# A decoder block with its gradients on one core: the last zero fill is moved to the end of GpSimd's queue and split unevenly over the transfer engines

## The chip, the core and the metric

The kernel runs on one core of one Trainium2 chip. A core has five engines with queues of their own: TensorE (PE in the profile, PEld for its weight loads), VectorE (DVE), ScalarE (ACT), GpSimd (POOL) and SyncE (SP). Data moves between the chip's memory and the core's on-chip buffer through sixteen transfer engines, which the profile calls DMA engines. GpSimd, SyncE and ScalarE only issue transfers; the sixteen carry them out. The metric is the time of one execution on the device, in microseconds (us), lower is better.

## The reference, cut to what matters

The program computes a forward pass of one token and all its gradients:

```python
mod = silu(c) @ w_mod                       # six vectors: sa, ca, ga, sb, cb, gb
h = layernorm(x) * (1 + ca) + sa
x = x + ga * attention(h, k_cache, v_cache, wq, wo)   # the last 4096 of 65536 rows alone
h = layernorm(x) * (1 + cb) + sb
x = x + gb * ((sigmoid(h @ w_gate) * (h @ w_up)) @ w_down)
...
_out, _vjp = jax.vjp(_f, x, k_cache, v_cache, wq, wo, w_gate, w_up, w_down, c, w_mod)
_grads = _vjp(grad_out)
return (_out, *_grads)
```

What matters here is the size of what goes out. The caches have 4 groups of 65,536 rows of 128 numbers in bf16. Only the last 4,096 rows of each group are read, so the gradients of both caches, `out_2` and `out_3`, are zero in the other 61,440 rows of each of the eight groups. These zeros have to be written: 126 MB of the 186 MB that the kernel writes. The rest is the gradients of the weights, of the 4,096 rows of each cache group, and a few vectors.

## The kernel before

**Work.** Everything that is read is loaded once and kept on chip, and stages follow one another in an order written out by hand: the modulation vectors and the query, attention scores, the folded products of the value cache and `wo`, the feed-forward block over seven column blocks of 512 (`turn`, loop at L1172), its gradients, the gradients of `wo`, `w_up`, `w_gate`, `w_mod` (`sec`, `s2`), `wq` (`dwq_tile`), and last the cache gradients: `grad_kv` makes 32 tiles for `out_3` (L1431) and 32 for `out_2` (L1481), and `kv_store` writes them group by group, 1 MB each.

**Queues.** Nearly all transfers are issued by GpSimd, in program order. SyncE issues some loads, and in the last stage part of the stores (`tail = nc.sync`, L1464): six 512-KB stores of L1312, two 1-MB stores of L1308, and the last three of the four `out_2` stores at L1304. The first of those four is the last transfer on GpSimd's queue. Each transfer of GpSimd's queue uses one of eight semaphores in turn, so it is issued only when the transfer eight before it has landed.

**Zero fills.** The zeros are cut into 120 pieces of 1 MB. `zero(n)` issues the next n pieces on GpSimd, and the tables `Z_...` at L49 to L59 say how many go out at each place of the program; a last call at L1485 would issue whatever is left. In this kernel nothing is left there: the last piece goes out at L1332 (`Z_ROWS[1]`), between the stores of the `w_up` gradient and those of the `wo` gradient. A piece is written in one of four ways:

- L209: from `zeros`, 128 rows of 2,048 one-byte zeros in the on-chip buffer, widened to 4 bytes on the way, so each of 128 rows becomes 8 KB, and each transfer engine writes eight of them (64 KB);
- L203 (`big`): from a part of the outputs that has been zeroed already (`zero_src`) to the output, 72 pieces;
- L194 and L197 (`narrow_`), for six pieces: the cursor that says which transfer engine comes next is set back (L192), then a small transfer of 5 rows of 256 bytes twice over goes out, and then 960 KB in 60 x 2 rows. The eight rows left out are written at L412 and L415;
- L201 (`uneven`): for the pieces whose number is in `UNEVEN`, which is empty here, so that it is never used.

The piece's number is worked out as `119 - len(zleft)` after it has been taken from the list, so 119 is the last of the 120.

**Lines that the change and the steps touch:** L39 and L59 (the tables), L171 to L183 (`uneven`), L185 to L211 (`zero`), L1332 (old place), L1130 and L1265 (the stores before and after it), L1304, L1308 and L1312 (the last stores), L1485 (new place), and L1511, the waits and the barrier that close the program.

Of the kernel before, what the change touches and what calls it, by code (L numbers as in the profile page):

```python
# [35 lines left out]
KIB = 512  # L36
SKIP = 4
NARROW = (15, 45, 75, 93, 103, 113)
UNEVEN = ()  # L39

def spread(total, n):
# [13 lines left out]
Z_FOLD = (1, 1, 2, 3)  # L56
Z_FFN = [(1, 0, 1)] + [(1, 1, 1)] * 4 + [(0, 2)]
Z_HAND = (1, 2, 1, 1, 1)
Z_ROWS = (1, 1, 0, 0, 0, 0, 0, 0)  # L59
JT = 3  # L60
JV = KD - JT
@with_exitstack
def kernel(
# [44 lines left out]
    def vt(shape, name, dt=FP32):  # L108
        return pool.tile(shape, dt, name=name)
# [4 lines left out]
    ZW = 4096  # L114
    zeros = vt([P, ZW // 2], "zeros", FP8)
# [55 lines left out]
    def uneven(piece):  # L171
        parts, at = [], 0
        flat_f = piece.rearrange("i x -> (i x)").bitcast(FP32)
        nc.gpsimd.inc_swdge_sem([], [], mode="reset_dge_cursor")
        for n, x in ((7, 16), (34, 512), (6, 16), (68, 512)):
            parts.append(nc.gpsimd.dma_start(
                out=flat_f[at:at + 2 * n * x].rearrange("(t p x) -> p t x", t=2, p=n),
                in_=zeros[0:n, 0:x].rearrange("p (t x) -> p t x", t=1).broadcast_to([n, 2, x])))
            at += 2 * n * x
        left = P * ZW // 2 - at  # L180
        nc.gpsimd.dma_start(out=flat_f[at:].rearrange("(p x) -> p x", p=16),
                            in_=zero_src.rearrange("i x -> (i x)")[0:left // 2].bitcast(FP8).rearrange("(p x) -> p x", p=16))
        return parts[0]  # L183

    def zero(n, after=None, big=False):  # L185
        for _ in range(n):
            if len(zleft) <= keep[0]:
                return
            region, narrow_ = zleft.pop(0)
            first = None  # L190
            if narrow_:
                nc.gpsimd.inc_swdge_sem([], [], mode="reset_dge_cursor")  # L192
                n = nlen - ncount.pop()
                first = nc.gpsimd.dma_start(  # L194
                    out=rest[0:NS, 0:nlen * 128].rearrange("p (t x) -> p t x", t=2)[:, :, n * 64:(n + 1) * 64],
                    in_=zeros[0:NS, 0:64].rearrange("p (t x) -> p t x", t=1).broadcast_to([NS, 2, 64]))
                ins = nc.gpsimd.dma_start(  # L197
                    out=region[8:P, :].bitcast(FP32).rearrange("(t p) x -> p t x", t=2),
                    in_=zeros[0:60, :].rearrange("p (t x) -> p t x", t=1).broadcast_to([60, 2, ZW // 2]))
            elif 119 - len(zleft) in UNEVEN:  # L200
                first = ins = uneven(region)  # L201
            elif big and region.shape[0] == 1:
                ins = nc.gpsimd.dma_start(  # L203
                    out=as_rows(region, BIGP).bitcast(FP32),
                    in_=zero_src[:, 0:P * ZW // 4].rearrange("i (p x) -> (i p) x", p=BIGP).bitcast(FP8))
            else:
                if region.shape[0] == 1:
                    region = as_rows(region, P)
                ins = nc.gpsimd.dma_start(out=region.bitcast(FP32), in_=zeros[:, :])  # L209
            if after is not None:  # L210
                dep(first or ins, after)  # L211
# [128 lines left out]
    def bcast(col_bf, ncols, out_bf, engs):  # L340
        for k, j0 in enumerate(range(0, ncols, 4)):
            ps = new_ps("bc_ps")
            for jj in range(4):
                nc.tensor.matmul(ps[:, jj * P:(jj + 1) * P],
                                 lhsT=col_bf[:, j0 + jj:j0 + jj + 1].broadcast_to([P, P]), rhs=ident_bf[:, :],
                                 start=(jj == 0), stop=(jj == 3), skip_group_check=True)
            o = out_bf[:, j0 * P:(j0 + 4) * P]
            if engs[k % len(engs)] == "A":
                last = nc.scalar.copy(out=o, in_=ps[:, :])
            else:  # L350
                last = cp(o, ps[:, :])
        return last
# [774 lines left out]
    def dw_rows(k, j, off, outer):  # L1127
        t = ar(off, 7)
        outer(t, h2[:, j:j + 1], dug_row[k])
        nc.gpsimd.dma_start(out=(dwu_view, dwg_view)[k][:, j, :], in_=t)  # L1130
# [94 lines left out]
    dw_rows(0, 1, 16, outer_dve)  # L1225
    zero(Z_ROWS[0])
    bcast(dattn_bf, KD, dattn_b, "V")
# [34 lines left out]
    def dwo(u):  # L1262
        for a in range(4):
            outer_dve(wo_t[u][:, a, :], o_perm[:, 8 * a + u:8 * a + u + 1], dattn_b)
        nc.gpsimd.dma_start(out=wo_dram(out_5, u), in_=wo_t[u])  # L1265
# [50 lines left out]
    for b in range(2):  # L1316
        do4 = new_ps("do4")
        for i in range(KD):
            for a in range(4):
# [4 lines left out]
                       in_=do4.rearrange("q (a h r) -> q a h r", a=4, h=4))  # L1324
# [6 lines left out]
    dw_rows(0, 2, 40, outer_dve)  # L1331
    zero(Z_ROWS[1])  # L1332
    dwo(2)
# [14 lines left out]
    dw_rows(0, 4, 32, outer_dve)  # L1348
    zero(Z_ROWS[2])
    dwo(3)  # L1350
    dw_rows(0, 5, 176, outer_dve)
    dw_rows(0, 6, 160, outer_dve)
    zero(Z_ROWS[3])
    dw_rows(0, 7, 40, outer_dve)
# [10 lines left out]
    dw_rows(1, 0, 64, outer_dve)  # L1365
    zero(Z_ROWS[4])
    dw_rows(1, 1, 72, outer_dve)
# [9 lines left out]
    dw_rows(1, 2, 80, outer_dve)  # L1377
    zero(Z_ROWS[5])
    dw_rows(1, 3, 88, outer_dve)
# [136 lines left out]
```

## Time and profile before

| | |
|---|---|
| median of 3 runs | 594.59 us (594.49 to 595.41) |
| the profiled execution | 594.85 us |
| its span in the profile | 593.0 us |
| busy: PE, DVE, ACT, POOL | 425.7, 354.7, 248.1, 145.9 us |
| moved in all | 246.58 MB, mean 416 GB/s |
| zero fills of L209, issue to landing | 42 of 1,024 KB, median 12.5 us |
| last issue on GpSimd, on SyncE | 560.75, 565.72 us |

The span is what the trace covers; the execution's own time is 1.85 us longer. The page divides the span into 40 equal slices and gives a digit for each engine: its busy share in tenths. The row DMA is the mean over the sixteen transfer engines. A queue's share in the table of queues is the time of its packets against sixteen engines' span; packets of one engine can overlap, so shares can add to more than the whole, and a stage's share can pass 1.00. In rows of the timeline come the start, the time taken, the engine, the line, the operation, and in brackets how long the engine stood idle before and what ended that. A group row gives the shortest, median and longest duration in ns and the first and last start. The trace also holds completion marks: for each transfer, the moment at which each of the sixteen engines reported its part as landed.

### The profile page before, as it was taken

The page shows a single profiled execution, that of the slowest core. Times are in us where ns is not written, and L with a number is a line of the kernel's source. Part 1 is how long each engine was busy: PE and PEld are TensorE (multiplying, and loading weights), DVE is VectorE, ACT ScalarE, POOL GpSimd, SP SyncE. Part 2 cuts the span into 40 slices and gives each one's busy share as a digit, 9 for nine tenths or more (in the row PEclk, how much of TensorE's full clock was granted, in tenths as well). Part 3 has the DMA queues.
Part 4 walks back from the last instruction along what each step waited for, and adds up shares of the span by engine and source line. Part 5 has one row for each costly group of instructions (what it writes and reads, how often), then busy time and mean ns, then how long its engine had stood idle before and what let it go on. Part 6 is the DMA issues. An engine that isn't in the chain of part 4 may idle for free.

```text
span 593.0 us, 10218 instructions
## 1 busy us (share of the span) xinstructions
PE 425.7 (72%) x4196; PEld 244.2 (41%) x4196; DVE 354.7 (60%) x647; ACT 248.1 (42%) x398; POOL 145.9 (25%) x250
## 2 busy tenths in 40 slices
PE   3997679999999999997975756776665457555300
PEld 2784433322334545643443545555452345131000
DVE  3765679988830102039272866887986868678700
ACT  2479511554540103411133646665672455563200
POOL 3113213112122212122222412323222432332100
PEclk9998889999999999999997757777787657555555
DMA  8999999999999999999999999999999999999996
GB/s 347 421 420 421 423 465 426 424 426 424 425 405 456 425 438 421 408 418 439 423 395 411 420 410 408 397 409 409 423 421 428 424 424 423 418 422 415 417 416 289
DMA packets 32047, 246.58 MB, mean 416 GB/s; under 512 B 4781, under 2 KB 4781, under 8 KB 16688
## 3 DMA queue, kind: packets, MB, share of 16 engines
q0 software_dynamic: 26864, 225.46, 94.3%
q1 hardware_dynamic: 5088, 20.46, 9.6%
q8 instruction: 33, 0.54, 0.4%
q14 instruction: 14, 0.11, 0.1%
q10 hardware_dynamic: 48, 0.01, 0.0%
HBM read 79.17 MB, written 185.60 MB: 446 GB/s over the span
## 4 chain that ended last, share of the span: by engine, by line
DMA 40%; PE 23%; DVE 19%; issue 5%; ACT 5%; POOL 1%; ACTq 0%; DVEq 0%; POOLq 0%; SPq 0%
DMA out_dram<-out_dram 12%; DMA out_dram<-arena 11%; PE n_ps L737 9%; DVE arena L249 7%; DMA arena<-in_w_mod_dram 6%; DMA arena<-in_B_w_gate_dram 5%; DVE arena L253 4%; PE t_ps L685 4%; DVE scr L253 3%; DMA out_dram<-zeros 3%; DMA arena<-in_B_w_down_dram 3%; PE b_ps L796 2%; ACT arena L524 2%; DVE arena L236 2%; PE tp_k L503 1%
## 5 line engine op out<-in xcount | busy, mean ns | idle before, releaser
L796 PE MATMUL b_ps<-arena 128*128 128x512 bf16 x512 | 116.3, 379 | 1.1 <-ACT arena L940 1.1
L236 DVE TENSOR_TENSOR arena<-arena 128x2048 bf16<-128x2048 bf16 x64 | 77.7, 1224 | 9.0 <-PE n_ps L737 5.3
L940 ACT COPY arena<-tp_side 128x1024 bf16<-128x1024 bf16 x62 | 60.9, 1017 | 49.7 <-PE tp_side L939 48.9
L796 PEld LDWEIGHTS <-arena 128*128 128x128 bf16 x512 | 48.3, 98 | 56.6 <-issue 2.9
L737 PE MATMUL n_ps<-arena 128*128 128x512 bf16 x256 | 67.6, 388 | 3.6 <-DVE arena L236 3.3
L203 POOL DMA_DIRECT2D out_dram<-out_dram x72 | 35.6, 495 | 128.8 <-PE n_ps L737 52.4
L939 PE MATMUL tp_side<-ident_bf,arena 128*128 128x128 bf16 x496 | 50.6, 268 | 10.4 <-DVE arena L236 6.0
L939 PEld LDWEIGHTS <-arena 128*128 128x128 bf16 x496 | 41.7, 123 | 19.4 <-issue 8.9
L693 ACT CAST arena<-t_ps 128x512 bf16<-128x512 f32 x56 | 28.9, 598 | 39.9 <-PE t_ps L685 39.9
L253 DVE CUSTOM_DVE_ANT_0 arena<-arena,scr 128x1024 bf16<-128x1024 bf16 x35 | 40.8, 1220 | 0.2
L209 POOL DMA_DIRECT2D out_dram<-zeros x42 | 23.1, 554 | 55.0 <-DVE rows_all L236 25.1
L1295 PE MATMUL ps_kv<-arena 32*128 32x512 bf16 x64 | 25.2, 584 | 15.6 <-DVE arena L257 9.5
L253 DVE CUSTOM_DVE_ANT_0 scr<-arena,b1k 128x1024 bf16<-128x1024 bf16 x28 | 34.2, 1222 | 3.4 <-DMA arena<-in_B_w_down_dram 3.0
L1299 ACT ACTIVATE arena<-ps_kv 128x512 bf16<-128x512 f32 x48 | 25.0, 723 | 26.7 <-PE ps_kv L1295 17.1
L737 PEld LDWEIGHTS <-arena 128*128 128x128 bf16 x256 | 21.4, 99 | 35.8 <-issue 19.5
L249 DVE TENSOR_SCALAR arena<-arena,h 128x3584 bf16<-128x3584 bf16 (+1 forms) x24 | 28.3, 1192 | 12.0 <-DMA out_dram<-arena 12.0
L245 DVE CAST arena<-b_ps 128x512 bf16<-128x512 f32 x6 | 4.1, 692 | 48.8 <-PE b_ps L796 48.8
L685 PE MATMUL t_ps<-arena 128*32 128x512 bf16 x256 | 24.1, 399 | 2.8 <-ACT arena L760 2.8
L524 ACT COPY arena<-tp_wq 128x1024 bf16<-128x1024 bf16 x23 | 21.4, 1070 | 7.3 <-PE tp_wq L522 7.3
L1077 ACT COPY arena<-tp_ug 128x1024 bf16<-128x1024 bf16 x21 | 20.5, 1007 | 7.0 <-PE tp_ug L1076 7.0
L965 POOL DMA_DIRECT2D arena<-in_B_w_up_dram x14 | 10.7, 765 | 40.1 <-DVE dh2acc L253 26.7
L1295 PEld LDWEIGHTS <-arena 32*128 32x128 bf16 x64 | 6.8, 114 | 32.9 <-issue 32.0
(326 smaller groups left out, 664.4 us busy)
## 6 DMA issues: line engine op xcount, KB each, us to landing
out_dram<-zeros POOLq DMA_DIRECT2D x42, 1024.0 KB, 12.5
out_dram<-arena POOLq DMA_DIRECT2D x34, 1024.0 KB, 16.4
out_dram<-arena POOLq DMA_DIRECT2D x16, 896.0 KB, 17.1
arena<-in_A_wq_dram POOLq DMA_DIRECT2D x8, 1024.0 KB, 21.0
arena<-in_A_wo_dram POOLq DMA_DIRECT2D x8, 1024.0 KB, 13.8
arena<-in_w_mod_dram POOLq DMA_DIRECT2D x7, 1024.0 KB, 19.0
arena<-in_B_w_up_dram POOLq DMA_DIRECT2D x14, 512.0 KB, 9.9
arena<-in_B_w_gate_dram POOLq DMA_DIRECT2D x14, 512.0 KB, 14.6
```

Source lines behind the costliest of these rows:

```text
L203: ins = nc.gpsimd.dma_start(out=as_rows(region, BIGP).bitcast(FP32), in_=zero_src[:, 0:P * ZW // 4].rearrange("i (p x) -> (i p) x", p=BIGP ...
L236: return nc.vector.tensor_tensor(out=out, in0=a, in1=b, op=op)
L249: return nc.vector.tensor_scalar(out=out, in0=a, scalar1=s1, scalar2=None, op0=op0)
L253: return nc.vector.tensor_tensor_reduce(out=out, in0=w, in1=b, scale=1.0, scalar=0.0, op0=ALU.mult, op1=ALU.add, accum_out=acc)
L524: nc.scalar.copy(out=blk, in_=tp[:, :])
L685: nc.tensor.matmul(ps[32 * hh:32 * hh + 32, :].rearrange("p (j m) -> p j m", j=4), lhsT=N_sb[:, h * P + a:(h + 1) * P - 3 + a:4], rhs=a4[: ...
L693: nc.scalar.copy(out=o, in_=v)
L737: mm = nc.tensor.matmul(nbank[k][:, :], lhsT=k_nat[:, g, t_ * DH:(t_ + 1) * DH], rhs=vp[:, t_ % 2, 4 * k:4 * k + 4, :].rearrange("p h d -> ...
L796: mm = nc.tensor.matmul(bbank[p][k][:, :], lhsT=a4[:, p, h, :], rhs=wo_t[u][:, a, k * 512:(k + 1) * 512], start=(i == 0 and a == 0), stop= ...
L939: nc.tensor.transpose(tp[:, i * P:(i + 1) * P], blk[:, i * P:(i + 1) * P], ident_bf[:, :])
L940: nc.scalar.copy(out=blk if dst is None else dst, in_=tp[:, :])
L1295: nc.tensor.matmul(ps[:, :], lhsT=rows[r, t8 * P:(t8 + 1) * P], rhs=bd[r, :], start=True, stop=True, tile_position=(32 * tc_, 0))
```

## The change

Three places change. The fill at `Z_ROWS[1]` is left out at L1332, so one piece is still in the list at the end, and the call at L1485 issues it behind all other entries of GpSimd's queue. That piece has number 119, which is now in `UNEVEN`, so it goes through `uneven`. And `uneven` itself is cut in another way.

```diff
-UNEVEN = ()
+UNEVEN = (119,)
...
-Z_ROWS = (1, 1, 0, 0, 0, 0, 0, 0)
+Z_ROWS = (1, 0, 0, 0, 0, 0, 0, 0)
...
         nc.gpsimd.inc_swdge_sem([], [], mode="reset_dge_cursor")
-        for n, x in ((7, 16), (34, 512), (6, 16), (68, 512)):
+        for n, t, x in ((7, 2, 16), (2, 12, ZW // 2), (6, 2, 16), (4, 12, ZW // 2)):
             parts.append(nc.gpsimd.dma_start(
-                out=flat_f[at:at + 2 * n * x].rearrange("(t p x) -> p t x", t=2, p=n),
-                in_=zeros[0:n, 0:x].rearrange("p (t x) -> p t x", t=1).broadcast_to([n, 2, x])))
-            at += 2 * n * x
+                out=flat_f[at:at + t * n * x].rearrange("(t p x) -> p t x", t=t, p=n),
+                in_=zeros[0:n, 0:x].rearrange("p (t x) -> p t x", t=1).broadcast_to([n, t, x])))
+            at += t * n * x
         left = P * ZW // 2 - at
         nc.gpsimd.dma_start(out=flat_f[at:].rearrange("(p x) -> p x", p=16),
                             in_=zero_src.rearrange("i x -> (i x)")[0:left // 2].bitcast(FP8).rearrange("(p x) -> p x", p=16))
```

The piece goes out as a reset of the cursor and five transfers: 7 rows of two 64-byte parts, 2 rows of twelve 8-KB parts, 6 rows of two 64-byte parts, 4 rows of twelve 8-KB parts, and the remaining 457,088 bytes in 16 equal parts of 28,568 bytes, which are copied from `zero_src`. If rows go to successive transfer engines from engine 0 on, the first transfer takes engines 0 to 6, the second 7 and 8, the third 9 to 14, and the fourth 15, 0, 1 and 2. Those six write 96 KB and the sixteenth of the rest; the other ten write the sixteenth of the rest and at most some 64-byte parts.

## The prediction

> **What bounds the kernel now.** I read the page first (slices and queues), then the last microseconds by stage, then GpSimd's queue around the moved fill, and last the closing instructions.
>
> ```profile
> DMA  8999999999999999999999999999999999999996
> GB/s 347 421 420 421 423 465 426 424 426 424 425 405 456 425 438 421 408 418 439 423 395 411 420 410 408 397 409 409 423 421 428 424 424 423 418 422 415 417 416 289
> q0 software_dynamic: 26864, 225.46, 94.3%
> q1 hardware_dynamic: 5088, 20.46, 9.6%
> ```
>
> The sixteen transfer engines are busy from the first slice to the last but one; no compute engine is above 72%. The kernel ends when the last of the sixteen has written its last byte. GpSimd's queue (q0) carries 225 of 247 MB, SyncE's (q1) 20. Only the last slice is loose:
>
> ```profile
> 584.00:585.00 1.00, 0.00 (x0) 0.00 (x0) 0.00 (x0) 0.00 (x0) 0.00 (x0) 0.50 1.04 434
> 585.00:586.00 1.00, 0.00 (x0) 0.00 (x0) 0.00 (x0) 0.00 (x0) 0.00 (x0) 0.50 0.94 393
> 586.00:587.00 1.00, 0.00 (x0) 0.00 (x0) 0.00 (x0) 0.00 (x0) 0.00 (x0) 0.50 0.87 369
> 587.00:588.00 1.00, 0.00 (x0) 0.00 (x0) 0.00 (x0) 0.00 (x0) 0.00 (x0) 0.50 0.81 344
> 588.00:589.00 1.00, 0.00 (x0) 0.00 (x0) 0.00 (x0) 0.00 (x0) 0.00 (x0) 0.50 0.43 180
> 589.00:590.00 1.00, 0.00 (x0) 0.00 (x0) 0.00 (x0) 0.00 (x0) 0.00 (x0) 0.50 0.25 107
> 590.00:591.00 1.00, 0.00 (x0) 0.00 (x0) 0.00 (x0) 0.00 (x0) 0.00 (x0) 0.50 0.08 33
> ```
>
> The last two columns are the share of the sixteen engines and GB/s. From 585 to 591 the shares add up to 3.38 of 6 us: on average an engine is idle for the last 2.6 us. That is all that any balancing can win. Which engines are idle, the trace's completion marks tell: each transfer leaves one mark from each engine (in order of time, without the engine's number). The last transfer of GpSimd's queue (L1304, issued at 560.75) and the last of SyncE's (L1304, issued at 565.72):
>
> ```
> GpSimd 575.71 575.86 579.34 579.63 579.82 580.02 | 580.57 581.08 581.12 581.44 581.83 581.84 582.66 583.71 584.47 584.51
> SyncE  585.60 585.76 588.09 588.19 588.38 588.39 | 588.44 588.73 588.80 589.20 589.36 589.43 590.12 590.26 591.23 591.27
> ```
>
> Six engines lead. They already do at the old place of the fill, where the L1130 store before it has marks at 464.70 to 465.19 for six and 466.02 to 468.77 for ten. At the end the six are through by 588.39 (mean 587.4), the ten by 591.27 (mean 589.7). From the last mark to the end of the span are 1.77 us of closing waits.
>
> **Does the change feed those six?** Its pieces go to positions 7, 8, 15, 0, 1, 2 if, as the code's narrow fills suppose, a transfer of n rows takes the next n engines from a cursor that was reset to engine 0. At the narrow fill of 328 us the trace has five pairs of 256-byte pieces (L194, engines 0 to 4): three are followed by marks of the leading six (335.14, 335.95, 336.45), two by marks of the ten. In its 960-KB part (L197, which skips engine 4) the mark without 64 KB before it is one of the ten. So three of the six are among engines 0 to 3, as wanted of 0, 1, 2; for 7, 8 and 15 only the count fits (three of the six are outside 0 to 4).
>
> **The change part by part.** *Removed:* the fill at L1332, the L209 row in
>
> ```profile
> 458.62 0.61 POOL L1130 DMA_DIRECT2D out_dram<-arena  x1 [3.58 <-DVE arena L249]
> 459.23 0.80 POOL L209 DMA_DIRECT2D out_dram<-zeros  x1
> 460.20 0.62 POOL L1265 DMA_DIRECT2D out_dram<-arena  x1 [0.18 <-issue]
> 530.38 0.53 POOL L1304 DMA_DIRECT2D out_dram<-arena  x1 [1.66 <-DMA out_dram<-arena]
> 551.39 0.90 POOL L1308 DMA_DIRECT2D out_dram<-arena  x1 [1.92 <-DVE arena L249]
> 560.75 0.53 POOL L1304 DMA_DIRECT2D out_dram<-arena  x1 [8.46 <-DVE arena L249]
> ```
>
> It costs each engine 64 KB: its first mark is 2.45 us after that of the store before (464.70 to 467.15), its last 2.46 (468.77 to 471.23). The 44 transfers behind it on GpSimd's queue move up by 2.45 us; so do SyncE's 14 behind 536 us, because the stores wait for DVE, and DVE waits for buffers that these transfers free. No engine runs dry: when L1265 is issued at 460.20, the earliest engine still has work until 464.70. So this is worth nothing by itself: the same 1 MB follows later.
>
> *Added:* behind the last store (560.75, then about 558.3) a cursor reset (18 ns on its six earlier occasions) and five issues at 0.53 to 0.67 us each (rows L209, L194, L197), some 3 us of GpSimd, beside 30 us of transfers. Each waits for the transfer eight before it: the 530.38 row starts 0.28 us after the last mark of that one (530.10). For the fourth and fifth that is 570.29 and 573.15, less 2.45: they are issued near 568 and 571. GpSimd's queue holds work on the earliest engine until 575.71 less 2.45 = 573.3, and SyncE's beyond 583: hidden. Without that cover an engine would stand idle for up to the 2.9 us between those two marks.
>
> Engine time, six engines: 12 pieces of 8 KB at the fill's own rate, 96/64 x 2.45 = 3.68; a sixteenth of the rest, 28,568 bytes at the 2.43 us which a 64-KB piece of L203 takes, 1.06; less 2.45: **+2.29 us**. Ten engines: 1.06 - 2.45 = **-1.39 us**. Four extra transfers on every engine: an L194 transfer leaves marks 0.16 to 0.24 us after those before it where it carries nothing, but L194 and L197 together took 2.45 us on the first engine at 424 us (430.88 to 433.33), no more than one full transfer. So between 0 and 0.8 us; I take 0.1, since the pair is the nearest row. Small pieces out of few partitions: L412 (23 KB per engine from 16 partitions) took 0.93 us where the fill's rate gives 0.86; at worst 8% of 3.68, 0.3 us, on the six; I take 0.
>
> The six then end at 588.39 + 2.29 + 0.1 = 590.8, the ten at 591.27 - 1.39 + 0.1 = 590.0. The six are now last, the end moves from 591.27 to 590.8: **-0.5 us**. With both bounds against it, 588.39 + 2.29 + 0.8 + 0.3 = 591.8, +0.5. The span would be 592.5 and its execution 594.85 - 0.5 = 594.35. That execution stands 0.26 above the median of the runs, so the time is 594.59 - 0.5 = **594.1**.
>
> [...]
>
> **The rivals.**
> *The ten set the end* (593.2). If the six take up part of their extra 60 KB beside SyncE's queue and gain more than 0.8 us on my sum, the end is the ten's, 591.27 - 1.39: 594.59 - 1.39. For it: at GpSimd's last transfer the lead is 4.4 us in the mean, against 2.3 at SyncE's, so the lead depends on how the two queues share an engine; and the shares above 1.00 show pieces that overlap. Against it: engines that have only one queue left move 64 KB in 2.45 us too.
>
> *GpSimd's closing drain becomes the last* (596.2, slower).
>
> ```profile
> L1511 SPq EVENT_SEMAPHORE  x11: 17/28/28, 576.6 to 593.0; - x11
> L1511 POOLq DRAIN  x3: 51/102/26978, 560.7 to 592.8; - x3
> ```
>
> The long drain runs from 560.73 to 587.71, 3.2 us beyond the last mark of GpSimd's queue (584.51); SyncE's own waits end at 592.2. Today 4.5 us of room. The change puts GpSimd's pieces last on six engines. If they land with SyncE's last, near 590.7, the drain ends at 593.9, 1.7 us beyond 592.2: 594.59 + 1.6. It decides once GpSimd's last mark is beyond 589. Against it: at half shares (64 KB took 4.85 us on the earliest engine, 570.86 to 575.71) the four later of the six need 577.6 + 7.4 + 2.1 = 587.1.
>
> *One of the six fed engines is not a leading one:* 591.27 + 2.29 = 593.56, so 596.9. Against it: the three leading engines found among 0 to 3. This is also how the change would not do what it says.
>
> *The middle runs dry without the fill:* at most its 2.45 us come back, 594.1 + 2.45 = 596.5; against it the 4.5 us of stock at 460.20.
>
> *Each small transfer takes the slot of a full one* (603.9): the engine waits for each transfer's mark before it begins the next, so four more cost four spacings of 2.45 us: 594.1 + 9.8. L194's marks all but exclude it. [...]
>
> **Chances.** Forecast 0.52, own range 593.3 to 595.1 (both bounds, and run to run differences of the tail); the ten set the end 0.23; the drain 0.10; a wrong engine 0.09; a dry middle 0.04; a slot each 0.02. A measurement tells about 0.2% (1.2 us) from no change: faster is below 593.4, slower above 595.8. Faster: 0.20 of the second case (some of it lies nearer) and 0.07 of the forecast's lower edge, 0.27. Slower: drain, wrong engine, dry middle, a slot each, less 0.02 of the drain that costs under 1.2 us: 0.23. Same: 0.50. The range reaches to 592.8, the second case with 0.4 us of slack, and to 596.3, which takes in the drain and half of the dry middle; it leaves out the wrong engine and the slot each.
>
> **What would show it.** Right: SyncE's last transfer has its six leading marks up by over 2 us against the ten's and a total spread of under 3 us (5.67 now); the DMA share stays near 1 until about 589 and falls at once; L1304 on GpSimd starts near 558.3; the marks of the ten end near 590. Wrong: a lone mark beyond 592 (a wrong engine), a drain of GpSimd that ends behind SyncE's waits, stores that start later than 558.3 plus 1 us (nothing moved up), or small transfers of the fill whose marks are 2 us apart.

## The result, and the profile after

| | before | after |
|---|---|---|
| median | 595.0 us of 4 runs (594.49 to 595.49) | 603.06 us of 4 runs (602.62 to 603.52) |
| ratio | | 1.0136 (95% interval 1.0118 to 1.0153) |
| the profiled execution, its span | 594.85, 593.0 us | 603.52, 601.5 us |
| last mark of GpSimd's queue | 584.51 | 597.38 |
| last mark of SyncE's queue | 591.27 | 596.31 |
| end of the span behind the last mark of all | 1.8 us | 4.1 us |

The changed kernel is 1.4% slower, about 8 us, where 0.5 us less was forecast. The bytes are the same, but the table of the page that counts packets is not. First the page of the kernel before, then that of the changed one (the row DMA is the busy share of the sixteen engines in tenths, in 40 slices):

```profile
DMA packets 32047, 246.58 MB, mean 416 GB/s; under 512 B 4781, under 2 KB 4781, under 8 KB 16688
```

```profile
DMA  8999999999999999999999999999999999999992
GB/s 353 420 417 421 424 451 438 418 429 413 442 427 439 415 423 441 433 406 419 419 434 377 421 406 397 405 413 410 421 425 424 427 421 412 422 413 412 412 407 87
DMA packets 32447, 246.58 MB, mean 410 GB/s; under 512 B 5221, under 2 KB 5221, under 8 KB 17128
q0 software_dynamic: 27264, 225.46, 93.1%
```

Up to the last slice little has changed: 407 GB/s in the 39th, against 416. The last slice moves 87 GB/s where it moved 289. And there are 400 packets more, all on GpSimd's queue (26,864 to 27,264). The changed kernel from 586 to 598 us by stage (the last two columns are the share of the sixteen engines and GB/s):

```profile
586.00:588.00 2.00, 0.00 (x0) 0.00 (x0) 0.00 (x0) 0.00 (x0) 0.00 (x0) 0.50 1.05 399
588.00:590.00 2.00, 0.00 (x0) 0.00 (x0) 0.00 (x0) 0.00 (x0) 0.00 (x0) 0.50 0.50 195
590.00:592.00 2.00, 0.00 (x0) 0.00 (x0) 0.00 (x0) 0.00 (x0) 0.00 (x0) 0.50 0.29 100
592.00:594.00 2.00, 0.00 (x0) 0.00 (x0) 0.00 (x0) 0.00 (x0) 0.00 (x0) 0.50 0.06 25
594.00:596.00 2.00, 0.00 (x0) 0.00 (x0) 0.00 (x0) 0.00 (x0) 0.00 (x0) 0.50 0.11 39
596.00:598.00 2.00, 0.00 (x0) 0.00 (x0) 0.00 (x0) 0.00 (x0) 0.00 (x0) 0.50 0.00 0
```

A share of 0.06 is one engine of sixteen. So fifteen engines are through near 592.6, and one writes on for another 5 us. The starts of its 8-KB packets show what it still has on both queues, and that these take turns on it one for one:

```
SyncE   591.25 591.87 592.50 593.12 593.74 594.36 594.98
GpSimd  591.60 592.22 592.84 593.46 594.09 594.71 595.33
```

Each takes 0.32 to 0.35 us, where 0.31 is the usual time in the kernel before, so by then this engine is hardly slow any more: it is behind. The completion marks say the same on both queues (in order of time, one per engine, without its number):

```
SyncE, last transfer  586.71 587.22 587.35 587.37 587.40 588.22 588.26 589.12 589.16 589.25 589.30 589.66 591.03 591.05 591.54 596.31
GpSimd, fill part 1   575.64 576.22 579.00 579.50 579.55 579.62 579.66 579.74 579.85 580.46 581.01 582.58 582.61 582.81 582.85 583.03
GpSimd, fill part 2   577.92 582.63 582.66 582.89 583.16 583.28 583.32 583.67 584.04 584.79 586.30 586.39 586.42 586.65 586.71 588.29
GpSimd, fill part 4   586.11 586.88 587.05 587.39 587.53 587.55 587.57 588.41 588.44 589.31 589.36 589.45 591.24 591.25 591.73 596.49
GpSimd, fill part 5   587.78 587.81 588.31 588.43 588.46 588.50 588.74 589.34 589.40 590.25 590.28 590.37 592.10 592.14 592.59 597.38
```

Two things stand in these rows. The lone engine is late with SyncE's store too (596.31 against 591.54), so it is that engine that is behind and not only its part of GpSimd's queue. And part 2, which has pieces for two engines alone, took 3.6 to 3.8 us of most of the others (580.46 to 584.04 and 582.58 to 586.30, for example, matched in order of time, with the marks of part 2 one place on).

The issues of the changed kernel on GpSimd's timeline (start, us, engine, line, operation, in brackets the idle time before):

```profile
558.15 0.53 POOL L1304 DMA_DIRECT2D out_dram<-arena  x1 [7.79 <-DVE arena L249]
558.75 0.60 POOL L176 DMA_DIRECT2D out_dram<-zeros  x1
560.01 0.63 POOL L176 DMA_DIRECT2D out_dram<-zeros  x1 [0.66 <-DMA out_dram<-arena]
564.31 0.54 POOL L176 DMA_DIRECT2D out_dram<-zeros  x1 [3.67 <-DMA out_dram<-arena]
568.02 0.64 POOL L176 DMA_DIRECT2D out_dram<-zeros  x1 [3.17 <-DMA out_dram<-arena]
571.09 0.53 POOL L181 DMA_DIRECT2D out_dram<-out_dram  x1 [2.44 <-DMA out_dram<-arena]
```

They are as forecast: the last store moved from 560.75 to 558.15, and the last piece is issued at 571.09, 4 us ahead of the first mark of that store. Nothing is late on the issuing side. The closing groups of the changed kernel (ns shortest, median and longest, then first and last start):

```profile
L1511 POOLq DRAIN  x3: 46/93/29672, 571.1 to 601.2; - x3
L1511 SPq DRAIN  x3: 7/7/7, 598.3 to 601.0; - x3
```

GpSimd's long drain begins behind its last issue and takes 29.67 us: to 600.74, 3.36 us behind the last mark of its queue. SyncE's own waits are over at 598.3. Before, the drain had ended 4.5 us ahead of them.

The span grew by 8.5 us: 5.0 by the lone engine (597.38 against 592.42, where it ends in the run `spread_rows` below, which lacks it), 1.1 from 591.27 to 592.42, and 2.4 behind the last mark (4.14 against 1.77).

### The profile page after: what moved, and what is told of

Its sections match the earlier page's. It is cut to its first block, busy times and chain, and to the rows that moved or that the text cites. A ratio compares the mean times of both kernels' runs of the same rounds, so it can differ in the third digit from the quotient of the medians.

```text
span 601.5 us, 10194 instructions
## 1 busy us (share of the span) xinstructions
PE 425.4 (71%) x4167; PEld 243.5 (40%) x4196; DVE 354.6 (59%) x647; ACT 248.0 (41%) x398; POOL 149.0 (25%) x254
## 3 DMA queue, kind: packets, MB, share of 16 engines
q0 software_dynamic: 27264, 225.46, 93.1%
## 4 chain that ended last, share of the span: by engine, by line
PE 39%; DMA 21%; DVE 20%; issue 7%; ACT 6%; POOL 2%; ACTq 0%; POOLq 0%; DVEq 0%
PE b_ps L796 14%; DMA out_dram<-arena 12%; PE n_ps L737 9%; DMA arena<-in_B_w_gate_dram 5%; DVE arena L236 4%; DVE arena L253 4%; PE t_ps L685 4%; DVE arena L249 3%; DVE scr L253 3%; DMA out_dram<-out_dram 3%; ACT arena L524 2%; PE tp_side L939 1%; PE tp_k L503 1%; PE w_ps L466 1%; PE fg L1053 1%
## 5 line engine op out<-in xcount | busy, mean ns | idle before, releaser
L737 PE MATMUL n_ps<-arena 128*128 128x512 bf16 x246 | 66.3, 389 | 3.8 <-DVE arena L236 3.0
L939 PE MATMUL tp_side<-ident_bf,arena 128*128 128x128 bf16 x496 | 48.7, 262 | 11.6 <-DVE arena L236 5.8
L1053 PE MATMUL fg<-arena,h_bf 128*32 128x256 bf16 x224 | 15.1, 404 | 7.3 <-DMA arena<-in_B_w_gate_dram 7.3
```

The lines of the kernel that those rows point to most:

```text
L737: mm = nc.tensor.matmul(nbank[k][:, :], lhsT=k_nat[:, g, t_ * DH:(t_ + 1) * DH], rhs=vp[:, t_ % 2, 4 * k:4 * k + 4, :].rearrange("p h d -> ...
L939: nc.tensor.transpose(tp[:, i * P:(i + 1) * P], blk[:, i * P:(i + 1) * P], ident_bf[:, :])
```

## Experiments

All kernels are variants of the changed one, and each diff is against it. Ratios are to the kernel before, run beside it on the same chip; "filler" is explained under `tiny_pieces`.

| run | what of the change is in it | median us | ratio, 95% interval | last mark GpSimd, SyncE |
|---|---|---|---|---|
| move_only | the move, even fill | 596.31 | 1.0022 (1.0012 to 1.0033) | 586.74, 591.01 |
| split_only | the five transfers at the old place | 597.93 | 1.0053 (1.0034 to 1.0072) | 587.50, 593.96 |
| before_store | all, ahead of the last store | 602.89 | 1.0133 (1.0115 to 1.0152) | 597.37, 596.46 |
| five_even | five transfers, even, no fillers | 596.90 | 1.0038 (1.0022 to 1.0054) | 588.62, 592.85 |
| one_piece | five transfers, even, from memory | 596.83 | 1.0034 (1.0021 to 1.0047) | 587.15, 591.41 |
| fat_pieces | uneven, few fillers, from memory | 596.56 | 1.0027 (1.0015 to 1.0039) | 588.34, 592.51 |
| tiny_pieces | even, all fillers | 599.38 | 1.0078 (1.0059 to 1.0096) | 593.12, 590.65 |
| spread_rows | all, other rows of `zeros` | 598.55 | 1.0062 (1.0047 to 1.0077) | 592.42, 591.37 |

Four more kernels held the fill back until SyncE's last store had landed; they show the fill alone, each was run once, and they are told below.

### Place or shape: move_only, split_only, before_store, isolated

The move without the new shape:

```diff
-UNEVEN = (119,)
+UNEVEN = ()
```

> The last fill goes to the end of GpSimd's queue, but in one even transfer (L209), as it was at its old place. Theory A (the split is at fault: in the changed kernel one transfer engine leaves its last marks at 596.49 and 597.38, the next one at 592.59): no lone late mark, the last fill's marks spread over less than 7 us, GpSimd's last mark before 589, time 593.5 to 595.5. Theory B (the place is at fault: whatever stands last on GpSimd's queue lands late beside SyncE's stores, and GpSimd's drain ends 3.3 us behind its last mark): GpSimd's last mark beyond 592, time above 599.

Measured: 596.31 us (594.56 to 597.09, 10 runs), 0.22% slower, and no lone mark: SyncE's last marks run from 586.20 to 591.01 and none stands alone at the end (590.64, 590.69, 591.01), and GpSimd's drain ends 3.2 us behind 586.74 and so ahead of SyncE's waits. So moving the fill costs some 1.5 us (theory A's range is missed by 0.8), and it isn't what makes the 8 us. Where the 1.5 us come from stays open: the execution that was profiled took 594.56, the fastest of the ten, and shows no reason.

The new shape at the old place:

```diff
-Z_ROWS = (1, 0, 0, 0, 0, 0, 0, 0)
+Z_ROWS = (1, 1, 0, 0, 0, 0, 0, 0)
```

> The last fill stays at its old place (L1332) and is cut into the five uneven transfers there. Theory A: the engine with too much is behind from then on, every later transfer of the queue lands late on it, time 598 to 602. Theory B: nothing small is at the tail, the drain ends before SyncE's waits as before, time 593.5 to 596.

Measured: 597.93 us, and neither theory had this. No engine is late at the end, nor behind the fill (part 5 has marks from 466.59 to 470.96, in line with the store before it, 464.57 to 468.87). SyncE's queue moves no packet there between 422 and 543 us, so the fill meets no second queue; whether that is why the source rows cost nothing there wasn't tried. The timeline of GpSimd at the old place shows a third thing:

```profile
459.30 3.29 POOL L176 DMA_DIRECT2D out_dram<-zeros  x4
462.58 0.77 POOL L181 DMA_DIRECT2D out_dram<-out_dram  x1
464.88 0.59 POOL L1265 DMA_DIRECT2D out_dram<-arena  x1 [1.54 <-DVE arena L249]
467.30 0.77 POOL L1265 DMA_DIRECT2D out_dram<-arena  x1 [1.82 <-DVE arena L249]
469.41 2.88 POOL L1265 DMA_DIRECT2D out_dram<-arena  x1 [1.35 <-DVE arena L249]
```

The stores of L1265 were issued at 460.20, 461.79 and 463.47 in the kernel before. They come 4.7 to 5.9 us later. The brackets name DVE, but each starts 0.54 to 0.60 us behind the last mark of the transfer eight before it (464.28, 466.73, 468.87): the five small transfers have taken five of the eight places that the queue has in flight, where in the kernel before the place for 460.20 had been free since 454.99. In the stage from 470 to 472 us the DMA share is 0.95 at 397 GB/s, against 1.00 at 414 before: in the middle of the program the stock does run thin. SyncE's last store goes out at 568.38, 2.7 us later than the 565.72 before, which is most of the 3.1 us. Ahead of work that still has to be issued, these five transfers cost more than one; that their number does it, and not their shape, is argued from the eight places, since five even transfers were not run there.

The fill one store earlier, so that a 1-MB store and not the fill is the last entry of the queue:

```diff
+    keep[0] = 0
+    zero(len(zleft))
     for g in range(G):
         kv_store(out_2, dk_home, g, nc.gpsimd if g < 1 else tail)
-    keep[0] = 0
-    zero(len(zleft))
```

> The uneven fill is issued just ahead of the out_2 store (L1304), not behind it, so that GpSimd's queue ends with an even store. Theory A: same load of each engine, time 600 to 604. Theory B: the fill's small transfers run while GpSimd waits for that store's data, its last mark comes before 589, the drain is covered, time 594 to 597.

Measured: 602.89 us, the changed kernel's time, and again one engine alone: 596.46 on SyncE's queue, the next at 591.17. So being the very last entry isn't the cause.

The fill by itself: `zero` is handed SyncE's last store and waits for it.

```diff
-        queue.dma_start(out=kv_out(og, g), in_=home[:, g, :])
+        return queue.dma_start(out=kv_out(og, g), in_=home[:, g, :])
...
-        kv_store(out_2, dk_home, g, nc.gpsimd if g < 1 else tail)
+        last_store = kv_store(out_2, dk_home, g, nc.gpsimd if g < 1 else tail)
...
-    zero(len(zleft))
+    zero(len(zleft), last_store)
```

> The changed kernel, with the uneven fill held back until SyncE's last store has landed, so that it runs alone and its marks show what each engine carries. If six engines have 12 pieces each (theory B, the split does what it says): two engines late by about 3.7 us in the second transfer, four others by about 3.7 us in the fourth, all sixteen within 5 us of each other at the end. If one engine is in both (theory A): one mark about 7.4 us behind the ten that have none. Time 600 to 606 by either.

Measured: 606.1 us in one run. Its timeline on GpSimd, and its last stages:

```profile
590.15 2.42 POOL L176 DMA_DIRECT2D out_dram<-zeros  x4 [30.59 <-DMA out_dram<-arena]
592.54 0.56 POOL L181 DMA_DIRECT2D out_dram<-out_dram  x1
```

```profile
594.00:596.00 2.00, 0.00 (x0) 0.00 (x0) 0.00 (x0) 0.00 (x0) 0.00 (x0) 0.50 0.49 162
596.00:598.00 2.00, 0.00 (x0) 0.00 (x0) 0.00 (x0) 0.00 (x0) 0.00 (x0) 0.50 0.30 115
598.00:600.00 2.00, 0.00 (x0) 0.00 (x0) 0.00 (x0) 0.00 (x0) 0.00 (x0) 0.50 0.11 41
```

With the other queues empty the marks show what each part does:

```
part 1  591.65 ... 591.78 (all sixteen)
part 2  592.35 ... 592.55 (fourteen)                596.13 596.27
part 4  593.54 ... 593.68 (ten)  596.58 596.64      597.64 598.24 599.03 599.13
part 5  595.24 ... 595.59 (ten)  597.20 597.34      598.68 599.30 600.09 600.18
```

Two engines write in part 2 and four others in part 4, so no engine is fed twice: a double load is out. But the two need 3.7 us for their twelve pieces, as forecast (3.68), and the four need between 4.0 and 5.5 from 593.6 on (the expectations below say 4.2 to 5.9).

On the engines without pieces the marks of part 2 come 0.7 us behind those of part 1. The expectations of `tiny_pieces` and `isolated_spread` take this for the price of a transfer of twelve pieces. It is the pace of the issues, which are 0.60 us apart (590.15 and 590.75): the 4-byte packets that part 2 leaves on these engines all start between 591.97 and 592.28, and from 591.49 to 591.95 no packet starts at all. The price without a second queue stands in `split_only`, where the transfers wait in a full queue of GpSimd's and SyncE's is empty: there part 2 comes 0.16 to 0.22 us behind part 1 on the engines without pieces, matched in order of time (464.76 to 464.94 and 469.04 to 469.22, for example).

### What the fillers are: tiny_pieces, five_even, fat_pieces, one_piece

In the changed kernel's trace, the parts that go to fewer than sixteen engines leave fillers, packets of 4 bytes. If there is one on each engine without a piece for each piece that the others get, parts 1 to 4 leave 9 x 2 + 14 x 12 + 10 x 2 + 12 x 12 = 350. With 16 completion packets for each of four more transfers that is 414, and the 4-byte packets of GpSimd's queue went from 4,065 to 4,479, by exactly 414. The same number of packets with 64 bytes in place of 8 KB makes the load of the engines even and keeps every filler:

```diff
-        for n, t, x in ((7, 2, 16), (2, 12, ZW // 2), (6, 2, 16), (4, 12, ZW // 2)):
+        for n, t, x in ((7, 2, 16), (2, 12, 16), (6, 2, 16), (4, 12, 16)):
```

> As the changed kernel, but the twelve pieces per row are 64 bytes, not 8 KB, and the last transfer takes the rest in 16 equal parts: every engine carries the same 64 KB, only the number of pieces is kept. In the isolated run each engine without pieces spent 0.7 us on a transfer of twelve pieces to others, so a transfer to few engines seems to put a short packet on every unused engine for each piece. Theory C (these filler packets cost): 414 more packets of 4 bytes than the kernel before, as in the changed kernel, all engines later by 2 to 4 us beside SyncE's stores, no single late engine, time 596.5 to 600. Theory D (the pieces' reads out of four neighbouring rows of the on-chip buffer collide with each other and with SyncE's reads on one engine): nothing left to collide, time within 1 us of the even fill at the end, 594.5 to 596.5.

Measured: 599.38 us. The lone engine is gone, but GpSimd's queue is now the last of all (593.12 against SyncE's 590.65). The counterpart has as many transfers, all of them on sixteen engines, and so no fillers:

```diff
-        for n, t, x in ((7, 2, 16), (2, 12, ZW // 2), (6, 2, 16), (4, 12, ZW // 2)):
+        for n, t, x in ((16, 1, ZW // 2),) * 4:
...
-                in_=zeros[0:n, 0:x].rearrange("p (t x) -> p t x", t=1).broadcast_to([n, t, x])))
+                in_=zeros[0:8 * n:8, 0:x].rearrange("p (t x) -> p t x", t=1).broadcast_to([n, t, x])))
```

> The last fill at the end of GpSimd's queue in five transfers as in the changed kernel, but each over all sixteen engines: four times one 8-KB piece per engine from every eighth row of the zeros, and the rest in 16 parts. No unused engine, so by theory C no filler packets: q0 has 64 packets of 4 bytes more than the kernel before (four completion packets per engine) and none beyond. Theory C: as the even fill in one transfer (move_only, 596.31), 595 to 597.5. [...]

Measured: 596.9 us. The closing groups of `tiny_pieces` and then of `five_even`, whose queues have 27,264 and 26,880 packets for the same bytes:

```profile
L1511 POOLq DRAIN  x3: 46/102/24540, 571.9 to 597.0; - x3
L1511 SPq DRAIN  x3: 7/7/7, 594.0 to 596.7; - x3
```

```profile
L1511 POOLq DRAIN  x3: 51/102/19902, 572.1 to 594.3; - x3
L1511 SPq DRAIN  x3: 7/7/7, 593.8 to 594.1; - x3
```

The long drain is the longest of its group: 24.54 us ends it at 596.48, 2.45 us after SyncE's first drain at 594.03; 19.90 us ends it at 591.98, ahead of SyncE's at 593.8. So 350 fillers, which carry 1.4 KB, put GpSimd's last mark 4.5 us later (593.12 against 588.62) and the median 2.5 us. The two also differ in how much they copy from memory, 64 KB for each engine against 32; `one_piece` below copies all of it from there and takes as long as `five_even`. Four more transfers by themselves cost 0.6 us against `move_only`, with intervals that overlap.

Fewer and larger pieces, copied from `zero_src`, so that the six still get 96 KB but the fillers are 90 in place of 350:

```diff
-        for n, t, x in ((7, 2, 16), (2, 12, ZW // 2), (6, 2, 16), (4, 12, ZW // 2)):
+        src = zero_src.rearrange("i x -> (i x)").bitcast(FP8)
+        for n, t, x in ((7, 2, 16), (2, 2, 12288), (6, 2, 16), (4, 2, 12288)):
...
-                in_=zeros[0:n, 0:x].rearrange("p (t x) -> p t x", t=1).broadcast_to([n, t, x])))
+                in_=src[0:t * n * x].rearrange("(t p x) -> p t x", t=t, p=n)))
```

> As the changed kernel with the same 96 KB more for each of the six engines, but in two pieces of 48 KB copied from the zeros in memory in place of twelve of 8 KB from the on-chip buffer. It takes away both: a transfer to few engines has two pieces, so few filler packets (64 x 1 + 18 + 28 + 20 + 24 more than the kernel before by theory C), and nothing is read from the on-chip buffer. Both theories: no lone late engine, the six and the ten end within 4 us of each other, as the prediction had it, time 593.5 to 596. If it stays above 600, both fall and the uneven load itself is at fault.

Measured: 596.56 us, with 4,219 4-byte packets (4,065 + 64 + 90). GpSimd's last mark is 588.34 and its drain is hidden. This is the cleanest trial of the balancing itself: the uneven load is there, and the lone engine and the drain are not. It is no faster than the even fill at the same place (596.31), it lies above the expected 593.5 to 596, and SyncE's last marks still run over 5.4 us (587.09 to 592.51, against 5.67 before) where 4 were expected.

The last of this group was to be the same with one 48-KB piece for each engine; against `fat_pieces`, only the loop's line differs:

```diff
+        src = zero_src.rearrange("i x -> (i x)").bitcast(FP8)
+        for n, t, x in ((7, 1, 16), (2, 1, 12288), (6, 1, 16), (4, 1, 12288)):
```

> As fat_pieces, but one piece of 48 KB for each of the six engines in place of two, and one 64-byte piece in the placing transfers: the six get 48 KB more than the ten, not 96. 45 filler packets (9 + 14 + 10 + 12) and 64 completion packets. Theory C and the marks (the six ahead by 2.3 us in the mean): six and ten end together within 4 us, the ten's last near 591.5, time 594.5 to 596.5; below 594.5 would be a version that beats the kernel before.

Measured: 596.83 us, but it isn't the case that it was built for. With one piece for each row the rows lie one behind the other in memory, and each transfer was cut into sixteen equal packets (16 each of 28, 6,144, 24, 12,288 and 47,052 bytes): no filler and no uneven load. It is a second `five_even` with another source, and its time agrees.

### Why one engine is late: spread_rows and the fill alone from other rows

Parts 2 and 4 read rows 0 and 1 and rows 0 to 3 of `zeros`. The same fill, read from rows 16, 20 and 0, 4, 8, 12:

```diff
-        for n, t, x in ((7, 2, 16), (2, 12, ZW // 2), (6, 2, 16), (4, 12, ZW // 2)):
+        for n, t, x, lo, step in ((7, 2, 16, 0, 1), (2, 12, ZW // 2, 16, 4), (6, 2, 16, 0, 1), (4, 12, ZW // 2, 0, 4)):
...
-                in_=zeros[0:n, 0:x].rearrange("p (t x) -> p t x", t=1).broadcast_to([n, t, x])))
+                in_=zeros[lo:lo + step * n:step, 0:x].rearrange("p (t x) -> p t x", t=1).broadcast_to([n, t, x])))
```

> As the changed kernel, but the pieces' sources are rows 16 and 20 of the block of zeros (two engines) and rows 0, 4, 8, 12 (four engines) instead of rows 0 and 1 and rows 0 to 3. Theory D (neighbouring rows collide): the long 8-KB packets (up to 0.76 us against 0.31) go, and with them the lone late engine; GpSimd's last mark before 593, time 595 to 598.5. Theory C: as the changed kernel, a last mark near 597, time 601.5 to 604.

Measured: 598.55 us, 4.5 us less than the changed kernel's 603.06. Its last stages, and then its closing groups:

```profile
590.00:592.00 2.00, 0.00 (x0) 0.00 (x0) 0.00 (x0) 0.00 (x0) 0.00 (x0) 0.50 0.24 82
592.00:594.00 2.00, 0.00 (x0) 0.00 (x0) 0.00 (x0) 0.00 (x0) 0.00 (x0) 0.50 0.01 4
594.00:596.00 2.00, 0.00 (x0) 0.00 (x0) 0.00 (x0) 0.00 (x0) 0.00 (x0) 0.50 0.00 0
```

```profile
L1511 POOLq DRAIN  x3: 46/93/25023, 570.8 to 596.3; - x3
L1511 SPq DRAIN  x3: 7/7/7, 593.3 to 596.0; - x3
```

From 592 on the share is 0.01: the lone engine is gone, and what it wrote is unchanged. The drain still ends 2.45 us behind SyncE's first (595.78 against 593.33). The rows were then tried with the fill alone, where nothing else reads. Each of the three kernels is `isolated` with other rows: 16, 20 and 0, 4, 8, 12; then 32, 33 and 0 to 3; then 16, 20 and 2 to 5.

> The isolated run with the rows of spread_rows. There, the fourth transfer took the four engines with pieces 4.2 to 5.9 us for 12 pieces, the second 3.7. Theory D: from rows 0, 4, 8 and 12 all six take 3.6 to 3.8 us. If the rows do not matter without SyncE's stores beside them: 4.2 to 5.9 again. The transfers of twelve pieces still cost each engine without pieces 0.7 us (theory C).

> Isolated run; the second transfer (two engines) reads rows 32 and 33, the fourth (four engines) rows 0 to 3. [...] Theory S (what collides is several engines reading the very same rows, 0 and 1, in both transfers): 3.6 to 3.8 us, no packet above 0.4 us.

> Isolated run; the second transfer reads rows 16 and 20, the fourth rows 2 to 5. [...]

The last stages of `isolated_spread`, to be laid beside those of `isolated`:

```profile
594.00:596.00 2.00, 0.00 (x0) 0.00 (x0) 0.00 (x0) 0.00 (x0) 0.00 (x0) 0.50 0.58 213
596.00:598.00 2.00, 0.00 (x0) 0.00 (x0) 0.00 (x0) 0.00 (x0) 0.00 (x0) 0.50 0.24 90
598.00:600.00 2.00, 0.00 (x0) 0.00 (x0) 0.00 (x0) 0.00 (x0) 0.00 (x0) 0.50 0.01 4
```

| run | rows of part 2, part 4 | the four engines of part 4 are through | longest 8-KB packet of the fill | one run, us |
|---|---|---|---|---|
| isolated | 0, 1 and 0 to 3 | 597.64 598.24 599.03 599.13 | 1.116 us | 606.1 |
| isolated_32 | 32, 33 and 0 to 3 | 598.04 598.62 599.42 599.52 | 1.116 us | 606.49 |
| isolated_spread | 16, 20 and 0, 4, 8, 12 | 597.24 597.25 597.27 597.42 | 0.348 us | 604.38 |
| isolated_2to5 | 16, 20 and 2 to 5 | 597.21 597.23 597.24 597.55 | 0.348 us | 604.53 |

Rows 32 and 33 are as bad beside rows 0 to 3 as rows 0 and 1 are, so the rows need not be the same. Rows 2 to 5 are neighbours and do no harm, so they need not be far apart. Rows 0 to 3 were not run with part 2 on other rows, but the packets tell that four readers are not enough: the nine packets of `isolated` over 0.35 us all start between 593.36 and 595.70, while part 2's engines read too, and behind the last mark of part 2 (596.27) none of the four's takes longer than 0.348. What would fit all four runs is a limit that rows 0 to 3 and 32 and 33 have in common and that rows 4, 5, 16 and 20 do not fall under; what it is, no trace shows. Measured is its price: from 593.6 on the four needed up to 5.5 us in `isolated`, and 3.6 to 3.9 in `isolated_spread` and `isolated_2to5`.

## Why the prediction was wrong

**The bound and the issues were right.** The transfer engines are the bound up to the last slice, the middle didn't run dry when the fill was moved: the last store was issued at 558.15 where 558.3 was forecast, and the fourth and fifth issue came at 568.02 and 571.09 where 568 and 571 were. The rival with a dry middle is right of the split at the old place only.

**"Small pieces out of few partitions" was the dearest term.** It was taken as 0 with 0.3 us as the worst, from L412, which reads from 16 partitions. The fill reads from four. The term measured 5.0 us of span (`spread_rows`: 592.42 against 597.38) and 4.5 us of the median. That the rows are the cause is shown. Why one engine alone ends so late beside SyncE's stores is not: it is late on SyncE's queue too (596.31), but the marks carry no engine's number, and in the fill alone, without SyncE's stores, the same rows cost only some 1.7 us (599.13 against 597.42).

**"Four extra transfers" was mis-sized next.** It was 0.1 us with 0.8 as the worst, from L194, whose transfers carry two pieces for each row. The cost goes by pieces and not by transfers: parts 2 and 4 have twelve. Between part 1 and part 2 most engines without pieces lost 3.6 to 3.8 us. Twelve turns of one filler against one 8-KB packet of SyncE's at 0.31 us (2.45 / 8) would be 3.7; that a filler takes a whole turn is inferred from this count, from the turns of the last engine's 8-KB packets, and from the 0.16 to 0.22 us that the same twelve fillers took where SyncE's queue was empty (`split_only`). The fillers cost 2.5 us of the median (`tiny_pieces` against `five_even`).

**The rival with GpSimd's drain was right in its mechanism** and was given a chance of 0.10. Its condition, a last mark of GpSimd's queue beyond 589, was met in `tiny_pieces`, `spread_rows` and `before_store` (593.12, 592.42 and 597.37) and in the changed kernel (597.38), and not in the other five of the table. Its price was too low: 1.6 us forecast, 2.4 measured, since it was worked out for a mark near 590.7, ahead of SyncE's end; where GpSimd's mark is the last of all, the price is the drain's 3.36 us less the 0.9 that SyncE's waits take behind the same mark. The argument against it, 587.1 at half shares, left out that the fillers wait beside SyncE's packets.

**The gain that all this was set against did not come.** The forecast said that the six end at 590.8 and the ten at 590.0, and that SyncE's marks spread over less than 3 us. Without the lone engine they spread over 4.8 us (586.71 to 591.54), and over 5.4 in `fat_pieces`, where neither source rows nor drain are in the way and the time is not below that of the even fill. The rival in which the ten set the end needed them at 589.9, and failed with it (its lead of 4.4 us at GpSimd's last transfer is 3.9 by the marks shown). The row that both start from was read for too much: only two of the six stand apart in SyncE's last marks (585.60 and 585.76, then 588.09), and the sixth is 0.05 us ahead of the seventh. At the old place the lead was there, and the fill took it: in `split_only` seven marks of the store before the fill stand ahead (464.57 to 465.54, then 466.83), and of the fill's last part one (466.59, then 468.12). Whether other engines lead at the end, or whether the order of the engines shifts when the queue in front of them changes, the marks can't tell; it stays open.

**The move was not worth nothing.** `move_only` took 596.31 us, 0.22% more; the cause is open, as said.

**A wrong engine** as a rival would also have left a lone mark, near 593.6 and not at 597.4. `isolated` shows each engine in one part only, and `spread_rows` removes the lone mark without changing which engines are fed. That the reset starts the count at engine 0 stays the code's supposition; without engine numbers no run shows it.

**A slot for each transfer** came to 603.9 us and is the nearest of all numbers to 603.06, by chance: `five_even` has as many transfers and takes 596.9; the four more cost 0.6 us against `move_only`.

The move, the four transfers, the fillers and the rows come to 1.5 + 0.6 + 2.5 + 4.5 = 9.1 us one by one, and 8.1 were measured; some of these steps lie between runs whose intervals overlap, so the difference isn't told apart. No kernel of these beat the one before.

## What to carry to other kernels

Before transfers are shaped to feed a few engines, count the packets on every engine of every part, the 4-byte ones too, and take the price from a row with as many pieces, as few source partitions and a second queue as full, not from the nearest by size. Where several engines read small sources at the same time, try other rows: here part 4 was through at 597.42 from rows 0, 4, 8, 12 and at 597.55 from rows 2 to 5, both beside rows 16 and 20, and at 599.13 from rows 0 to 3 beside 0 and 1. And know which queue's closing wait takes longer: GpSimd's, whose drain ended 3.2 to 3.4 us behind its last mark here, should not be the one that ends last.

## Hardware behaviour that was not expected

- The narrow GpSimd transfers of this fill cost the engines that they do not use: 350 packets of 4 bytes in all, by the count one for each piece. Twelve took 0.16 to 0.22 us where SyncE's queue was empty (`split_only`), and 3.6 to 3.8 us beside it (the changed kernel).
- With part 2 read from rows 0 and 1 and part 4 from rows 0 to 3, some of the 8-KB packets took 0.456 to 1.116 us (`isolated`); with part 2 from rows 16 and 20 and part 4 from 0, 4, 8, 12 or from 2 to 5 the longest took 0.348 (`isolated_spread` and `isolated_2to5`).
- GpSimd's closing drain ended 3.2 to 3.4 us behind the last mark of its queue in the kernel before, the changed kernel and each variant whose drain was read, whether that mark was at 584.51 or at 600.18. SyncE's waits were over 0.9 us behind the last mark of either queue (592.20 against 591.27 in the kernel before, 598.29 against 597.38 in the changed one).
- The transfers of `one_piece`, written as 7, 2, 6 and 4 rows that lie one behind the other in memory, were cut into sixteen equal packets each (28, 6,144, 24 and 12,288 bytes).
